# Feature sums of the first batch from a masked operand, and more of its outer products on GpSimd

## The chip, the cores and the metric

The kernel runs on one core of a Trainium2 chip. The metric is the device time of one execution in microseconds (us), the median of several runs. Engines are called as the profile calls them: PE (TensorE), DVE (VectorE), ACT (ScalarE), POOL (GpSimd), SP (SyncE, which only issues transfers here).

## The reference

Two layers, one behind the other. The first is an attention whose features are products of two small projections; the second is a gated feed-forward layer on its output.

```python
# q, k, v: (4, 4, 1088, 32); S1, S2: (8, 32)
def phi(x):
    a = np.einsum('rd,bhsd->bhsr', S1, x)
    b = np.einsum('rd,bhsd->bhsr', S2, x)
    return np.einsum('bhsi,bhsj->bhsij', a, b).reshape(*x.shape[:-1], r * r)
q_p, k_p = (phi(q), phi(k))
kv = np.einsum('bhsf,bhsd->bhfd', k_p, v)
z = np.sum(k_p, axis=2)
num = np.einsum('bhsf,bhfd->bhsd', q_p, kv)
den = np.einsum('bhsf,bhf->bhs', q_p, z)[..., None] + 1e-06
attn_out = num / den
# x: attn_out as (4352, 128)
gate = 1.0 / (1.0 + np.exp(-(x @ w_gate)))      # w_gate, w_val: (128, 1536)
out = (gate * (x @ w_val)) @ w_out              # w_out: (1536, 128)
```

The 64 features of a key are the outer product of its two projections a and b of 8 values each. z, the sum of these features over the 1088 keys of a head, is what the change computes in another way. S1, S2 and the weights arrive as 64-bit numbers and are narrowed to float32 on the chip.

## The kernel before

**Two phases that overlap.** The feed-forward layer is worked off in chunks of 512 tokens; each chunk is a sequence of twelve "waves" (`w1`, L501: gate and value products of one 128-wide slice of d_ff), each followed by the sigmoid on ACT (L509), the product g on DVE (L540) and, some waves later, the output products (L382, L338). The attention of batches 1 to 3 is put between the waves. The attention of batch 0 has nothing to hide behind: the first wave needs its result, so it stands alone at the start. All the code that the change touches belongs to this run-in of batch 0, apart from a few constants made ahead of it.

**What sets the order.** PE, DVE, ACT and POOL run under a manual schedule: every engine works through its instructions in the order in which the code emits them, and waits at each one for the semaphores of what it reads and of what it overwrites. So the place of a call in the source is its place in each engine's queue. Transfers are issued by SP, and a few by ACT.

**The run-in of batch 0, in the code's order.**
- `turn_k` transposes the keys; `kps(0)` projects them on PE, and DVE transposes the result back, for each pair of heads `pi` (L640, tile kab): 128 partitions of tokens, `NJK` = 9 token columns, and for each of the two heads of a pair the 8 values of a and the 8 of b.
- `ab` projects the queries on PE (tiles aps and bps); ACT copies one of the two (asb, L747), and `mult00` and `mult10` multiply them on DVE into qp (L756; one operand is in PSUM).
- `gram` multiplies kab by itself on PE: since z is the sum over the keys of a times b, z is the 8x8 block of kab-transposed times kab. The products of 9 token columns and two pairs go into PSUM tile gram (bank acc0). ACT copies 64 columns to gs (L662). POOL multiplies them by a mask e_m into gh, 128 x 32 (L664). `spread_z` then sums with one PE matmul against the constant e_sum (128 x 128; L676), which leaves every partition with a whole row of products; `mask_z` picks from it on DVE with the mask m_col (zm, L687) and a reduction (zb, L699). zb is z, in the layout that the denominator's matmul wants.
- `outer` forms the 64 features of the keys, kp, from kab by a product with two broadcast operands (L709), both in SBUF. Token column 8 of both pairs is made on POOL, behind gh; columns 0 to 4 by DVE; columns 5 to 7 by DVE after zb.
- `warm(512)` is a matmul of constants behind `spread_z` in PE's order (L260).
- `dn(0, 0, rest)`: PE computes the denominators dps from zb and qp (L1020). `rest` then has `kv0` (L836: kv from v and kp), the last DVE outers, the transpose dT of dps (L1031), the copy rc on ACT, and the turn of kv into nd (L871, L905, L922). The numerators nps follow (L1039), then the reciprocal, rb and the product xT (L1055 to L1060), which the first wave reads.
- `narrow` and `narrow_01` narrow the weights in steps on ACT (tail, L101; square, L117), POOL (cap, L97; head, L118) and DVE (head, L105 and L109; w_sb, L127), emitted between the steps above.

The calls that order this are in the main body:

```python
kps(0)
ab((0, 0, 0))
ab((0, 1, 0))
spread_z, mask_z = gram()
mult00 = ab(None, (0, 0, 0))
mult10 = ab(None, (0, 1, 0), (psm, "wave"))
```

Of the kernel before, what the change touches and what calls it, by code (L numbers as in the profile page):

```python
# [8 lines left out]
F32 = mybir.dt.float32  # L9
# [3 lines left out]
ALU = mybir.AluOpType  # L13
ACTF = mybir.ActivationFunctionType
MUL = ALU.mult

P = 128
# [3 lines left out]
def kernel(  # L21
# [12 lines left out]
    nc = tc.nc  # L34
# [234 lines left out]
    ident = const.tile([P, P], F32, tag="ident")  # L269
    make_identity(nc, ident)  # L270

    e_sum = const.tile([P, 2, R, R], F32, tag="e_sum")
    e_row = const.tile([P, R], F32, tag="e_row")
    e_m = const.tile([P, 2], F32, tag="e_m")
    id_m = ident.rearrange("p (g m x) -> p g m x", g=4, m=2)[:, :, :, :R]

    m_col = const.tile([P, 2, R], F32, tag="m_col")
    nc.gpsimd.memset(m_col, 0.0)
    for c in range(2):
        rows = slice(64 * c, 64 * c + 64)  # L280
        nc.vector.tensor_reduce(
            out=m_col[rows, c],
            in_=ident[rows].rearrange("p (k j) -> p j k", j=R),
            axis=mybir.AxisListType.X,
            op=ALU.add,
        )
    for t, x in (
        (e_row, id_m.rearrange("p g m x -> p x g m")),
        (e_m, id_m.rearrange("p g m x -> p m g x")),
    ):  # L290
        nc.vector.tensor_reduce(out=t, in_=x, axis=mybir.AxisListType.XY, op=ALU.add)
    nc.vector.tensor_copy(
        out=e_sum,
        in_=bass.AP(
            tensor=e_row.tensor,
            offset=e_row.offset,
            ap=[list(e_row.ap[0]), [0, 2], [1, R], [0, R]],
        ),
    )
    eps = const.tile([P, 1], F32, tag="eps")  # L300
    nc.gpsimd.memset(eps, 1e-6)
    zb = const.tile([P, H, 32], F32, tag="zb", name="zb")
# [317 lines left out]
    def kps(b):  # L620
        t = ps2.tile([P, 2, 512], F32, tag="two", name="kps")
        ts = [t[:, 0], t[:, 1]]
        turns = [(g, pi) for g in range(4) for pi in range(2)]

        if b == 0:
            ts[1] = pso.tile([P, TCH], F32, tag="acc1", name="kps1")
            turns.sort(key=lambda x: x[1])
        for g, pi in turns:
            rows = slice(64 * pi, 64 * pi + 64)
            nc.tensor.matmul(  # L630
                out=ts[pi][32 * g : 32 * g + 32, : NJK * 32],
                lhsT=sk[rows, :],
                rhs=kT_of[b][rows, KBASE[g] : KBASE[g] + NJK],
                start=True,
                stop=True,
            )

        KAB[b] = sbA.tile([P, 2, NJK, 32], F32, tag="kab", name="kab")
        for pi in range(2):
            nc.vector.transpose(  # L640
                out=KAB[b][:, pi].rearrange("p j c -> p (j c)"), in_=ts[pi][:, : NJK * 32]
            )
        KP[b] = sbA.tile([P, 2, NJK, 2, F], F32, tag="kp", name="kp", bufs=1)
# [3 lines left out]
    def gram():  # L647
        t = pso.tile([P, TCH], F32, tag="acc0", name="gram")
        for pi in range(2):
            for j in range(NJK):  # L650
                g = 32 * (j % 4)
                x = KAB[0][: 64 if j == 0 else P, pi, j]
                nc.tensor.matmul(
                    out=t[g : g + 32, 32 * pi : 32 * pi + 32],
                    lhsT=x,
                    rhs=x,
                    start=(j < 4),
                    stop=(j >= NJK - 4),
                    skip_group_check=True,
                )  # L660
        gs = const.tile([P, 2, 2, 2, R], F32, tag="gs")
        nc.scalar.copy(out=gs.rearrange("p a m x r -> p (a m x r)"), in_=t[:, :64])  # L662
        gh = const.tile([P, 2, 2, R], F32, tag="gh")
        nc.gpsimd.tensor_tensor(  # L664
            out=gh,
            in0=gs[:, :, :, 1],
            in1=bass.AP(
                tensor=e_m.tensor,
                offset=e_m.offset,
                ap=[list(e_m.ap[0]), [0, 2], [1, 2], [0, R]],  # L670
            ),
            op=MUL,
        )

        def spread_z():
            nc.tensor.matmul(  # L676
                out=t[:, 64 : 64 + H * R],
                lhsT=e_sum.rearrange("p c i j -> p (c i j)"),
                rhs=gh.rearrange("p a m r -> p (a m r)"),
                start=True,  # L680
                stop=True,
            )

        def mask_z():
            zm = const.tile([P, H, 2, R], F32, tag="zm")
            z0 = t[:, 64 : 64 + H * R]
            nc.vector.tensor_tensor(  # L687
                out=zm,
                in0=bass.AP(
                    tensor=z0.tensor, offset=z0.offset, ap=[list(z0.ap[0]), [R, H], [0, 2], [1, R]]  # L690
                ),
                in1=bass.AP(
                    tensor=m_col.tensor,
                    offset=m_col.offset,
                    ap=[list(m_col.ap[0]), [0, H], [R, 2], [1, R]],
                ),
                op=MUL,
            )
            nc.vector.tensor_reduce(  # L699
                out=zb[:, :, :2], in_=zm, axis=mybir.AxisListType.X, op=ALU.add  # L700
            )

        return spread_z, mask_z


    def outer(b, pi, j0=0, j1=NJK, eng=nc.vector):
        a0 = KAB[b][:, pi, j0:j1]
        ap = [list(a0.ap[0]), [2 * R, 2 * (j1 - j0)]]
        eng.tensor_tensor(  # L709
            out=KP[b][:, pi, j0:j1].rearrange("p j m (i l) -> p (j m) i l", i=R),  # L710
            in0=bass.AP(tensor=a0.tensor, offset=a0.offset, ap=ap + [[1, R], [0, R]]),
            in1=bass.AP(tensor=a0.tensor, offset=a0.offset + R, ap=ap + [[0, R], [1, R]]),
            op=MUL,
        )
# [6 lines left out]
    def ab(a_of=None, b_of=None, pool_b=None):  # L721

        mm = []
        if a_of is not None:
            aps = psm.tile([P, 2, 512], F32, tag="wave", name="aps")
            mm.append((a_of, aps, sa))
        if b_of is not None:
            pool, tag = (ps2, "two") if pool_b is None else pool_b
            bps = pool.tile([P, 2, 512], F32, tag=tag, name="bps")
            mm.append((b_of, bps, sb))  # L730
        for c in range(2):
            for m in range(2):
                for (bb, pr, n), dst, sx in mm:
                    h = 2 * pr + m
                    rows = slice(32 * h, 32 * h + 32)
                    t0, tn = q_chk[n]
                    nc.tensor.matmul(
                        out=dst[64 * c : 64 * c + 64, m, : 32 * tn],
                        lhsT=sx[rows, :],
                        rhs=qT_of[bb][rows, t0 : t0 + tn, c, :],  # L740
                        start=True,
                        stop=True,
                    )
        if a_of is not None:
            w = 32 * q_chk[a_of[2]][1]
            ASB[a_of] = sbA.tile([P, 2, 256], F32, tag="asb", name="asb", bufs=2)
            nc.scalar.copy(out=ASB[a_of][:, :, :w], in_=aps[:, :, :w])  # L747
        if b_of is not None:

            def mult():  # L750
                bb, pr, n = b_of
                if bb not in QP:
                    QP[bb] = sbA.tile([P, 2 * H * W1], F32, tag="qp", name="qp")
                t0, tn = q_chk[n]
                w = 32 * tn
                nc.vector.tensor_tensor(  # L756
                    out=half(QP[bb], n).rearrange("p (m c) w -> p c m w", m=2)[:, pr],
                    in0=bps[:, :, :w],
                    in1=ASB[b_of][:, :, :w],
                    op=MUL,  # L760
                )

            return mult
# [372 lines left out]
    sa, sb = sab  # L1136
    turn_q(0, 0)
    kps(0)
    ab((0, 0, 0))
    ab((0, 1, 0))  # L1140
    spread_z, mask_z = gram()
    mult00 = ab(None, (0, 0, 0))
    mult10 = ab(None, (0, 1, 0), (psm, "wave"))
    for pi in range(2):
        outer(0, pi, NJK - 1, NJK, eng=nc.gpsimd)
    for part in range(2):
        narrow_01(part, 0)
    spread_z()
    warm(512)
    for pi in range(2):  # L1150
        outer(0, pi, 0, 5)
    mult00()
    mult10()
    mask_z()


    def rest(turn, rc, dT):
        kv0([1, 2, 3, 4, 0])
        for pi in range(2):
            outer(0, pi, 5, NJK - 1)  # L1160
        kv0(range(5, NJK))
        turn()
        nt = rc.shape[1] - 1
        nc.scalar.activation(out=rc[:, :nt], in_=dT[:, :nt, :2], func=ACTF.Identity, bias=eps)
        kvd(0)
        narrow_01(0, 1)
        narrow_01(0, 2)
        ndt(0)
# [189 lines left out]
```

## Time and profile before

| what | value |
|---|---|
| median of 3 runs | 294.37 us (293.91 to 294.39) |
| profiled execution | 295.29 us, its span 293.5 us |
| PE busy, share of the span | 286.3 us, 98% |
| DVE, POOL, ACT busy | 187.4, 160.4, 92.1 us |
| first wave (L501) starts | 14.93 us into the span |

The span runs from the first to the last instruction that the profile saw; the execution's own time is 1.79 us longer. Busy times are modelled for PE: matmuls overlap, so a busy PE is not one at its peak. A line of the timeline gives the start, the length, the engine and line, the operation, output and inputs with their shapes, how many of them are merged, and in brackets the idle time ahead of the first and what ended it.

### The profile page before, as it was taken

The numbers are of one execution on the slowest core, as the hardware profiler recorded it, in microseconds if no ns is written. First come the engines' busy times: TensorE is split into PE (matmuls) and PEld (weight loads), VectorE is DVE, ScalarE is ACT, GpSimd is POOL, SyncE is SP. The second block draws the span as 40 slices with busy tenths as digits, with TensorE's granted clock in tenths as the row PEclk, the third lists the DMA queues.
The fourth block names the chain that finished last, engine by engine and source line by source line (L and its number), as shares of the span: only waits on it lengthen the run. The fifth ranks groups of instructions, "written<-read, shape, count | busy, mean of one in ns | idle before, by whom it ended". The sixth has DMA issues, their size and how long they took to land.

```text
span 293.5 us, 5784 instructions
## 1 busy us (share of the span) xinstructions
PE 286.3 (98%) x2276; PEld 155.4 (53%) x2276; DVE 187.4 (64%) x320; ACT 92.1 (31%) x168; POOL 160.4 (55%) x221
## 2 busy tenths in 40 slices
PE   8899999999899999999999999999999999999995
PEld 3444433346355455554555555554555555555895
DVE  6998789964847766677556695667336423552482
ACT  3557532322223322423223223313223222322321
POOL 2465553995345657546446498655456565656300
PEclk9999999999999999999999999999999999999999
DMA  7994531594700148436000574202000200020002
GB/s 215 328 354 105 134 95 57 127 172 133 220 22 0 20 128 167 127 83 181 9 0 2 129 171 105 41 0 38 1 2 0 36 2 0 0 32 6 2 3 53
DMA packets 28890, 24.23 MB, mean 83 GB/s; under 512 B 18560, under 2 KB 24064, under 8 KB 28864
## 3 DMA queue, kind: packets, MB, share of 16 engines
q1 hardware_dynamic: 28352, 23.10, 31.1%
q10 hardware_dynamic: 512, 0.77, 0.9%
q8 instruction: 18, 0.29, 0.4%
q14 instruction: 8, 0.07, 0.1%
HBM read 20.60 MB, written 3.26 MB: 81 GB/s over the span
## 4 chain that ended last, share of the span: by engine, by line
PE 76%; DMA 15%; SPq 3%; DVE 3%; POOL 1%; issue 1%; ACT 0%; POOLq 0%
PE wave L501 49%; PE prod L338 20%; DMA bq<-dq 7%; DMA v<-in_v_dram 3%; DMA w_in<-in_moe_w_out_dram 2%; PE moeout L408 2%; POOL head L118 1%; DMA kq<-in_k_dram 1%; PE moeout L382 1%; SPq L801 1%; PE nps L1214 1%; SPq L157 1%; DMA dq<-cq 1%; PE kvz L849 1%; DVE w_sb L127 1%
## 5 line engine op out<-in xcount | busy, mean ns | idle before, releaser
L501 PE MATMUL wave<-xT,w_sb 128*64 128x512 f32 (+3 forms) x820 | 210.7, 566 | 0.1
L501 PEld LDWEIGHTS wave<-xT,w_sb 128*64 128x64 f32 (+1 forms) x820 | 85.7, 140 | 63.1 <-issue 48.6
L509 ACT ACTIVATE sg<-wave 128x512 f32<-128x512 f32 x102 | 60.9, 597 | 170.7 <-PE wave L501 169.5
L540 DVE TENSOR_TENSOR g<-wave,sg 128x512 f32<-128x512 f32 x96 | 65.9, 686 | 75.7 <-ACT sg L509 74.5
L328 POOL TENSOR_TENSOR tsum<-g 128x256 f32<-128x256 f32 x84 | 66.9, 798 | 31.6 <-DVE g L540 31.4
L328 POOL TENSOR_TENSOR tsum<-g,tsum 128x256 f32<-128x256 f32 x42 | 34.2, 814 | 57.4 <-DVE g L540 57.2
L338 PE MATMUL prod<-tsum,ws 128*64 128x256 f32 x252 | 62.8, 381 | 0.0
L338 PEld LDWEIGHTS prod<-tsum,ws 128*64 128x64 f32 x252 | 31.2, 137 | 16.2 <-issue 11.8
L338 PE MATMUL prod<-g,w_sb 128*64 128x256 f32 x168 | 34.9, 383 | 0.0
L328 POOL TENSOR_TENSOR tsum<-tsum,g 128x256 f32<-128x256 f32 x42 | 32.7, 779 | 3.3
L338 PEld LDWEIGHTS prod<-g,w_sb 128*64 128x64 f32 x168 | 15.7, 137 | 18.2 <-issue 15.4
L338 PE MATMUL prod<-tsum,w_sb 128*64 128x256 f32 x84 | 25.4, 384 | 0.0
L338 PE MATMUL prod<-g,ws 128*64 128x256 f32 x84 | 25.0, 379 | 0.0
L118 POOL TENSOR_TENSOR head<-head,tail 128x384 int32<-128x384 int32 (+2 forms) x14 | 13.3, 953 | 17.8 <-DVE head L109 11.6
L338 PEld LDWEIGHTS prod<-g,ws 128*64 128x64 f32 x84 | 11.5, 137 | 3.7
L829 DVE TENSOR_TENSOR qp<-qp,bq 128x1152 f32<-128x1152 f32 (+1 forms) x7 | 9.1, 1296 | 6.4 <-DMA a<-dq 6.4
L382 PE MATMUL moeout<-g,w_sb 128*128 128x512 f32 (+1 forms) x28 | 12.6, 607 | 0.3 <-DVE w_sb L127 0.3
L338 PEld LDWEIGHTS prod<-tsum,w_sb 128*64 128x64 f32 x84 | 10.9, 137 | 2.9 <-issue 1.9
L709 DVE TENSOR_TENSOR kp<-kab 128x1152 f32<-128x1152 f32 (+2 forms) x10 | 10.9, 1111 | 0.0
L440 DVE TENSOR_TENSOR res<-prod,other 64x512 f32<-64x512 f32 (+1 forms) x14 | 7.6, 543 | 3.1 <-ACT other L434 3.1
L533 DVE TENSOR_TENSOR g<-wave,sg 128x512 f32<-128x512 f32 x6 | 6.5, 1087 | 4.7 <-ACT sg L509 4.7
L475 DVE STREAM_TRANSPOSE o_sb<-res 64x512 f32<-64x512 f32 x14 | 9.5, 686 | 0.0
(121 smaller groups left out, 201.5 us busy)
## 6 DMA issues: line engine op xcount, KB each, us to landing
qp<-dq SPq DMA_DIRECT2D x7, 576.0 KB
bq<-dq SPq DMA_DIRECT2D x14, 288.0 KB
kq<-in_k_dram SPq DMA_DIRECT2D x3, 544.0 KB
kq<-in_q_dram SPq DMA_DIRECT2D x3, 544.0 KB
w_in<-in_moe_w_out_dram SPq DMA_DIRECT2D x6, 256.0 KB
w_in<-in_moe_w_gate_dram SPq DMA_DIRECT2D x5, 256.0 KB
w_in<-in_moe_w_val_dram SPq DMA_DIRECT2D x5, 256.0 KB
out_dram<-o_sb SPq DMA_DIRECT2D x20, 64.0 KB
```

Of the source, the lines that this page charges most:

```text
L118: nc.gpsimd.tensor_tensor(out=head, in0=head, in1=tail, op=ALU.add)
L328: nc.gpsimd.tensor_tensor(out=t[:, u], in0=in0, in1=in1, op=ALU.subtract)
L338: nc.tensor.matmul(out=out, lhsT=lhsT, rhs=rhs, start=start, stop=stop, skip_group_check=True)
L382: nc.tensor.matmul(out=moe["acc"][d], lhsT=w_sb[:, 2, j, d], rhs=g[:, jj], start=(j == 0), stop=(j == NJ - 1),)
L440: nc.vector.tensor_tensor(out=out, in0=in0, in1=in1, op=op)
L475: nc.vector.transpose(out=o_sb[:64, d].rearrange("p t x -> p (t x)"), in_=r[:, 1 + 2 * d : 3 + 2 * d].rearrange("p u x -> p (u x)"),)
L501: nc.tensor.matmul(out=wv[d, which, jj * tw + o : jj * tw + o + tp], lhsT=w_sb[:, which, j0 + jj, d], rhs=xT[:, t0 + o : t0 + o + tp], sta ...
L509: nc.scalar.activation(out=sg, in_=wv[:, 0], func=ACTF.Sigmoid)
L533: nc.vector.tensor_tensor(out=g.rearrange("p (j u s y) -> p j y u s", j=2, u=2, y=4), in0=wv[:, 1].rearrange("p (j y u s) -> p j y u s", j ...
L540: nc.vector.tensor_tensor(out=g, in0=wv[:, 1], in1=sg, op=MUL)
L709: eng.tensor_tensor(out=KP[b][:, pi, j0:j1].rearrange("p j m (i l) -> p (j m) i l", i=R), in0=bass.AP(tensor=a0.tensor, offset=a0.offset, ...
L829: nc.vector.tensor_tensor(out=q0, in0=q0, in1=half(BQ[b], n), op=MUL)
```

## The change

Three things are changed. gh becomes the whole masked operand: POOL spreads the 8 products of each head over 64 columns (i, j) with the mask e_row, and gh is 128 x 256 instead of 128 x 32. `spread_z` sums it by eight small matmuls, one for each head and half, with gh as the stationary operand and a constant e_c of two columns as the moving one; each writes 64 partitions and two columns. ACT copies these eight columns to zb, so zm, the reduction on DVE and the constants e_sum, e_m and m_col are gone. And POOL makes token columns 7 and 8 of kp instead of column 8 alone, ahead of gh in its order, straight behind `kps(0)`; DVE's last outers are columns 5 and 6. The call of `spread_z` now stands ahead of the first narrowing step, which puts the copy zb ahead of the tails (L101) in ACT's order.

```diff
-    e_sum = const.tile([P, 2, R, R], F32, tag="e_sum")
...
+    id_m = ident.rearrange("p (g m x) -> p m x g", g=4, m=2)[:, :, :R]
+    e_row = const.tile([P, 2, 2, R], F32, tag="e_row")
+    for a in range(2):
+        nc.vector.tensor_reduce(out=e_row[:, a], in_=id_m, axis=mybir.AxisListType.X, op=ALU.add)
+    e_c = const.tile([P, 2, 2], F32, tag="e_c")
+    nc.vector.memset(e_c, 0.0)
     for c in range(2):
...
+        nc.vector.memset(e_c[:, c, c : c + 1], 1.0)
...
-        gh = const.tile([P, 2, 2, R], F32, tag="gh")
+        gh = const.tile([P, H, R, R], F32, tag="gh")
+        g0 = gs[:, :, :, 1]
         nc.gpsimd.tensor_tensor(
             out=gh,
-            in0=gs[:, :, :, 1],
+            in0=bass.AP(
+                tensor=g0.tensor, offset=g0.offset, ap=[list(g0.ap[0]), [2 * R, H], [0, R], [1, R]]
+            ),
             in1=bass.AP(
-                tensor=e_m.tensor,
...
+                tensor=e_row.tensor,
+                offset=e_row.offset,
+                ap=[list(e_row.ap[0]), [R, H], [1, R], [0, R]],
             ),
             op=MUL,
         )
 
         def spread_z():
-            nc.tensor.matmul(
-                out=t[:, 64 : 64 + H * R],
-                lhsT=e_sum.rearrange("p c i j -> p (c i j)"),
...
-        def mask_z():
...
+            for h in range(H):
+                for c in range(2):
+                    nc.tensor.matmul(
+                        out=t[64 * c : 64 * c + 64, 64 + 2 * h : 66 + 2 * h],
+                        lhsT=gh[:, h].rearrange("p i j -> p (i j)"),
+                        rhs=e_c[:, c],
+                        start=True,
+                        stop=True,
+                        skip_group_check=True,
+                    )
+            nc.scalar.copy(
+                out=zb[:, :, :2], in_=t[:, 64 : 64 + 2 * H].rearrange("p (h c) -> p h c", c=2)
+            )
...
     kps(0)
+    for pi in range(2):
+        outer(0, pi, NJK - 2, NJK, eng=nc.gpsimd)
     ab((0, 0, 0))
     ab((0, 1, 0))
-    spread_z, mask_z = gram()
+    spread_z = gram()
     mult00 = ab(None, (0, 0, 0))
     mult10 = ab(None, (0, 1, 0), (psm, "wave"))
-    for pi in range(2):
-        outer(0, pi, NJK - 1, NJK, eng=nc.gpsimd)
+    spread_z()
     for part in range(2):
         narrow_01(part, 0)
-    spread_z()
     warm(512)
     for pi in range(2):
         outer(0, pi, 0, 5)
     mult00()
     mult10()
-    mask_z()
...
         for pi in range(2):
-            outer(0, pi, 5, NJK - 1)
+            outer(0, pi, 5, NJK - 2)
```

More of the change, by code (lines that the diff above doesn't have):

```diff
@@ L270 @@
     make_identity(nc, ident)
-    e_sum = const.tile([P, 2, R, R], F32, tag="e_sum")
[L273 to L278, printed above, removed]
-    for c in range(2):
[L280 to L299, printed above, removed]
+    id_m = ident.rearrange("p (g m x) -> p m x g", g=4, m=2)[:, :, :R]
[4 more added lines that the diff above has]
+    nc.vector.memset(e_c, 0.0)
+    for c in range(2):
+        nc.vector.memset(e_c[:, c, c : c + 1], 1.0)
     eps = const.tile([P, 1], F32, tag="eps")
@@ L662, in gram @@
         nc.scalar.copy(out=gs.rearrange("p a m x r -> p (a m x r)"), in_=t[:, :64])
-        gh = const.tile([P, 2, 2, R], F32, tag="gh")
+        gh = const.tile([P, H, R, R], F32, tag="gh")
+        g0 = gs[:, :, :, 1]
         nc.gpsimd.tensor_tensor(
             out=gh,
-            in0=gs[:, :, :, 1],
+            in0=bass.AP(
+                tensor=g0.tensor, offset=g0.offset, ap=[list(g0.ap[0]), [2 * R, H], [0, R], [1, R]]
+            ),
             in1=bass.AP(
-                tensor=e_m.tensor,
-                offset=e_m.offset,
-                ap=[list(e_m.ap[0]), [0, 2], [1, 2], [0, R]],
+                tensor=e_row.tensor,
+                offset=e_row.offset,
+                ap=[list(e_row.ap[0]), [R, H], [1, R], [0, R]],
             ),
@@ L675, in spread_z @@
         def spread_z():
-            nc.tensor.matmul(
-                out=t[:, 64 : 64 + H * R],
-                lhsT=e_sum.rearrange("p c i j -> p (c i j)"),
-                rhs=gh.rearrange("p a m r -> p (a m r)"),
-                start=True,
-                stop=True,
-            )
-        def mask_z():
[L685 to L703, printed above, removed]
+            for h in range(H):
[10 more added lines that the diff above has]
+                out=zb[:, :, :2], in_=t[:, 64 : 64 + 2 * H].rearrange("p (h c) -> p h c", c=2)
+            )
+        return spread_z
     def outer(b, pi, j0=0, j1=NJK, eng=nc.vector):
```

## The prediction

> **What bounds the kernel now.** I read the page's busy shares and slices first, then the busy time by stage, then the timeline of the stage that the change touches.
>
> ```profile
> PE 286.3 (98%) x2276; PEld 155.4 (53%) x2276; DVE 187.4 (64%) x320; ACT 92.1 (31%) x168; POOL 160.4 (55%) x221
> ```
>
> ```profile
> 6.80:10.80 4.00, 3.46 (x76) 1.59 (x74) 3.97 (x9) 1.97 (x5) 1.94 (x5) 1.00 1.11 299
> 10.80:15.00 4.20, 3.33 (x100) 1.99 (x100) 4.10 (x12) 2.42 (x7) 1.42 (x3) 1.00 1.03 349
> 15.00:22.50 7.50, 7.16 (x27) 3.40 (x28) 7.10 (x16) 4.01 (x8) 4.69 (x8) 1.00 1.06 345
> 22.50:48.00 25.50, 25.44 (x82) 10.51 (x84) 20.89 (x40) 12.57 (x25) 14.90 (x19) 1.00 0.39 109
> 100.00:200.00 100.00, 100.00 (x845) 53.67 (x842) 66.29 (x102) 28.94 (x50) 62.62 (x76) 1.00 0.37 86
> ```
>
> After each window's length stand the busy times of PE, PEld, DVE, ACT and POOL. From 22.5 us on PE has no holes, apart from 0.92 us at 74.4 to 75.8, where denj waits for a DMA. In the run-in, 6.8 to 15.0, VectorE is the full engine: 3.97 of 4.00 and 4.10 of 4.20 us. So whatever delays or advances the first wave (L501, at 14.93) moves the whole PE-bound rest with it, one to one. The waits of 15 to 22.5 are DVE, ACT, POOL and PE on each other; the last weight slices land some microseconds ahead of their use (w_in 2 at 16.5, first read at 20.3), so no transfer holds that stretch in place.
>
> The run-in on VectorE, POOL and PE (timeline of each engine):
>
> ```profile
> 7.55 1.52 DVE L709 TENSOR_TENSOR kp<-kab 128x640 f32<-128x640 f32 x2
> 9.05 1.29 DVE L756 TENSOR_TENSOR qp<-bps,asb 128x512 f32<-128x512 f32 x2
> 10.26 0.21 DVE L687 TENSOR_TENSOR zm<-gram,m_col 128x64 f32<-128x64 f32 x1
> 10.50 0.22 DVE L699 TENSOR_REDUCE zb<-zm 128x8 f32<-128x64 f32 x1
> 10.64 1.10 DVE L709 TENSOR_TENSOR kp<-kab 128x384 f32<-128x384 f32 x2
> 11.66 0.44 DVE L1031 STREAM_TRANSPOSE dT<-dps 128x256 f32<-128x256 f32 x1
> ```
>
> ```profile
> 9.22 0.41 PE L676 MATMUL gram<-gh,e_sum 128*128 128x32 f32 x2 [0.28 <-POOL gh L664]
> 9.46 1.11 PE L260 MATMUL warm<-const-float32-1.0 128*128 128x512 f32 x2
> 10.78 0.64 PE L1020 MATMUL dps<-qp,zb 128*32 128x256 f32 x8 [0.21 <-DVE zb L699]
> ```
>
> From dT (11.66) to the first wave, every step follows from dT: rc, its reciprocal, rb, the narrowing of w_sb, xT. VectorE is full from 11.66 to 14.88, so the shift of dT is the shift of the wave. dT needs both VectorE free and dps done; dps ends 0.64 after it starts, so dT can start 0.70 after dps starts. Today VectorE decides: dps would allow 11.48.
>
> **Who may use SBUF.** These POOL and DVE lines carry the forecast:
>
> ```profile
> 8.68 0.48 POOL L664 TENSOR_TENSOR gh<-gs,e_m 128x32 f32<-128x32 f32 x1 [2.43 <-ACT gs L662]
> 9.13 0.76 POOL L709 TENSOR_TENSOR kp<-kab 128x128 f32<-128x128 f32 x2
> ```
>
> ```profile
> 39.32 1.35 DVE L829 TENSOR_TENSOR qp<-qp,bq 128x1152 f32<-128x1152 f32 x1
> ```
>
> ```profile
> 39.57 1.96 POOL L118 TENSOR_TENSOR head<-head,tail 128x384 int32<-128x384 int32 x1 [1.12 <-DVE head L109]
> ```
>
> gh has 32 elements and yet takes 0.48 us, ending 0.10 after the DVE outer product ends (9.07). The add of 39.57 takes 1.96 where its like take 1.00, ending 0.86 after qp ends (40.67). In both, POOL stood still while DVE ran an operation with two SBUF operands. The two POOL outers of 9.13 run beside L756, which reads PSUM, and take 0.40 each, undisturbed. The other way round, L109 on DVE took 1.01 instead of 0.56 at 16.98 because a POOL add ran until 17.58. [...] the one held back ends about 0.13 early against its own length (0.86 for 1.00)[...].
>
> On length, [...] 0.592 us for 192 elements (L324) and 0.722 for 256 (L328), 2.03 ns per element. On matmuls, [...] here the last 16 gram passes start in fours, 32 ns apart.
>
> **The change, part by part.**
>
> *Set-up.* Of the DVE reductions m_col, e_row, e_m and the copy e_sum (1.45 us together), two reductions and three memsets remain; a POOL memset goes. Nothing: VectorE waits for s_in until 3.73 anyway, and is through at 2.69 today.
>
> *Off VectorE.* zm and zb (10.26 to 10.64) go, and the last outers fall from 384 to 256 elements: by 0.93 ns per element (0.784 for 640, 0.546 for 384) 0.12 each. Together 0.66 us less before dT, if dps lets dT come.
>
> *Onto POOL, ahead of gh.* Two outers of 256 elements instead of two of 128 behind gh, and gh itself is 256 instead of 32. Length of each: 0.40 plus 128 x 2.03 ns is 0.66; a plain 256 takes 0.727. I take 0.69, with 0.60 and 0.80 as ends. POOL follows DVE by 0.15 to 0.17 (L109 12.73, L118 12.88), so the first starts at 7.26 (first kab) + 0.16 = 7.42, ahead of the DVE outer at 7.55, and they share the lock:
> - POOL outer 1: 7.42 to 8.11. DVE outer 1, held until 8.11, ends at 8.11 + 0.78 - 0.13 = 8.76.
> - DVE outer 2 is issued before outer 1 ends. In such a case (o_sb and kp at 168 us) a waiting POOL add got the lock only after both. So DVE outer 2 ends at 8.76 + 0.74 = 9.50.
> - POOL outer 2 ends at 9.50 + 0.69 - 0.13 = 10.06; gh, beside the PSUM-reading L756, runs 10.02 to 10.71.
>
> Were POOL let in between the two DVE outers, gh would end at 10.54; were DVE first at 7.55, at 10.94. I take 10.71, against 9.17 today: 1.54 later. L756 moves by 0.43 and ends at 10.79, which nobody feels.
>
> *On PE.* One matmul (2 passes, 128 columns, loads 0.11 apart) becomes eight (16 passes of 64 columns). A 64-column load taken as half of 0.11, two column groups together: 8 x 0.055 = 0.44 us; ends 0.25 and 0.90 (no overlap). Behind it in PE's order stands warm (512 columns), then dps. Today the first warm pass starts 0.25 after the first gh load, and dps could follow 1.19 after that load; now it becomes 1.43. With gh at 10.71 the load starts at 10.76 and dps at 12.19, 1.41 later than today's 10.78.
>
> *zb.* Eight columns copied by ACT instead of two DVE steps, about 0.2 (gs takes 0.21), beside the 1.1 us of warm: nothing. Queued behind it on ACT are the two tails (L101), late by some 1.5 us; POOL's first head needs them only after dT. If that cover goes, the tails' 0.76 us would stand ahead of rc.
>
> *POOL's caps* (L97), now behind gh, move from 10.07 to 10.67 or later; DVE's L105 needs them after dT. Nothing. No DMA moves.
>
> *Sum.* dT at 12.19 + 0.70 = 12.89, against 11.66: +1.23. VectorE then idles ahead of dT: the 0.66 that it gained is lost in a wait for dps. The second path, kvz to nps, moves by 1.41 but has 0.25 of slack ahead of xT (nps over at 14.16, xT at 14.47): +1.16, just covered. The wave moves to about 16.16. The profiled execution would take 295.29 + 1.23 = 296.5 (its span is 293.5, 1.79 lie around it; it stands 0.92 above the median of the runs). From the median: 294.37 + 1.23 = 295.6. With lengths of 0.60, the early order and 0.25 for PE the shift is +0.6; with 0.80, the late order and 0.90 it is +2.2.
>
> **The rivals.**
>
> *No contention, faster.* If POOL's two outers ran beside DVE's, gh would end at about 7.42 + 3 x 0.66 - 0.07 = 9.33, dps start at 10.81 and dT at 11.51: -0.15, 294.2. With PE at 0.25 it is -0.34. It decides once gh ends before 9.3; it ends at -0.66 (293.7), where VectorE itself is the bound again, and that needs gh at 8.8. For it speaks that 0.66 us really leaves the full engine; against it stand gh's 0.48 and the 1.96 of L118.
>
> *Hidden later.* The shift is real at the first wave but the 0.92 us wait of denj takes it in: +0.3, 294.7. Against: its transfer starts from cq, which PE makes, so it moves too.
>
> *The PE clock.* PE would stand idle from 8.94 to 10.76. [...] the granted clock is 1.00 in every window today, so no trace here shows such a fall. [...]
>
> **How the numbers follow.** A measurement of this kernel can tell about 0.2% (0.59 us) from no change. Lock chain 0.81 (0.71 slower by more than that, 0.10 within it); no contention 0.13 (0.07 faster, where the POOL operations also turn out shorter than assumed, 0.06 within); hidden later 0.04 (0.03 within, 0.01 slower); clock 0.02, slower. Faster 0.07, same 0.19, slower 0.74. The range goes from just under the short ends of the chain to its long ones, 294.5 to 296.4; it leaves out most of the no-contention case and the clock.
>
> **What would show it.** Right: POOL outers or DVE outers of 1.2 us and more between 7.4 and 10; gh ending near 10.7; warm ending near 12.2; VectorE idle ahead of dT, released by PE dps; the first wave near 16.2; stages after 22.5 as long as now. Wrong: POOL and DVE outers both at their own length and gh over by 9.4, or a first wave before 15.

## The result, and the profile after

The changed kernel is slower: median 297.29 us of 16 executions, against 295.50 of 16 of the kernel before, ratio 1.0068 (95% interval 1.0046 to 1.0091). Run again beside the experiments it gave 297.63 against 295.03, ratio 1.0060 (1.0035 to 1.0084). Ratios are formed from the fast executions of both kernels, so they are not the quotients of the medians beside them. The profiled execution took 297.28, its span 295.5: 2.0 us more than before. The forecast was 295.6, in 294.5 to 296.4: the right direction, too small.

The timeline of each engine in the run-in, first POOL, then DVE, then PE (start, length, work, and in brackets the idle time ahead and what ended it):

```profile
8.11 1.79 POOL L679 TENSOR_TENSOR kp<-kab 128x256 f32<-128x256 f32 x2 [1.91 <-DVE kab L620]
9.86 1.20 POOL L645 TENSOR_TENSOR gh<-gs,e_row 128x256 f32<-128x256 f32 x1
11.03 0.79 POOL L97 TENSOR_SCALAR cap<-w_in 128x256 f32<-128x256 f32 x2
```

```profile
7.54 0.85 DVE L620 STREAM_TRANSPOSE kab<-kps 128x288 f32<-128x288 f32 x2 [1.10 <-PE kps L610]
8.31 2.27 DVE L679 TENSOR_TENSOR kp<-kab 128x640 f32<-128x640 f32 x2
10.50 1.27 DVE L726 TENSOR_TENSOR qp<-bps,asb 128x512 f32<-128x512 f32 x2
11.70 0.74 DVE L679 TENSOR_TENSOR kp<-kab 128x256 f32<-128x256 f32 x2
13.44 0.45 DVE L1001 STREAM_TRANSPOSE dT<-dps 128x256 f32<-128x256 f32 x1 [1.00 <-PE dps L990]
```

```profile
9.02 0.69 PE L707 MATMUL bps<-qT,s 32*64 32x256 f32 x16
11.11 0.63 PE L661 MATMUL gram<-e_c,gh 128*64 128x2 f32 x16 [1.41 <-POOL gh L645]
11.68 1.13 PE L260 MATMUL warm<-const-float32-1.0 128*128 128x512 f32 x2
12.73 0.64 PE L990 MATMUL dps<-qp,zb 128*32 128x256 f32 x8
```

The chain of the forecast is all there. Its first part is called the lock, or the port lock, here: a name for turns that the lengths show; what makes POOL and DVE take them was not shown. Where POOL ran beside the DVE outers, which have two SBUF operands, the two took turns: the two DVE outers take 2.27 us instead of 1.52, POOL's second outer takes 1.21 where its first takes 0.62, and gh 1.20. DVE, full before, stands idle for 1.00 ahead of dT, released by PE's dps; and dps stands behind gh, the sum and warm. PE itself has a hole of 1.41 ahead of the sum.

Before the chain begins, this execution is already later than the earlier profile: the first transpose kab starts at 7.54 instead of 6.78. Here PE ran slowly for longer: the two constant matmuls ahead of kps took 1.22 together, against 0.70, and the trace's record of the clock, whose first entry is 1.00, begins at 6.93 instead of 4.03. In two of the later profiles (the changed kernel again, and the one without warm) kab starts still later, at 7.74 and 7.76, for another reason: the transpose of the keys waited 0.90 and 0.88 for their transfer. In the others it starts at 6.8 to 7.1. Neither cause lies in code that was changed, but all three late starts are among the eight profiles with the new constants and none among the three with the old ones; so few don't exclude a link. I measure from the start of kab. dT comes 5.90 us after it, against 4.88 before: +1.02. xT, the first wave's input, comes 8.72 after it, against 7.69: +1.03. The profile's 2.0 us are these 1.03, the late start's 0.76, and some 0.36 of a longer wait of denj for its transfer, less small differences:

```profile
PE denj L948 <- DMA b<-dq: 1.3, 2, 0.8
```

(The waits of PE after 24 us: in total, times, longest; before it was 0.9, and over all the profiles it is 0 to 1.8.) One execution cannot say what the other half of the 2.0 is in all executions. The list of executions can: each has a mean granted PE clock, as a share of the full one. The values fall into two groups, 0.998 and more or 0.994 and less; one stretch of 3.41 us at a clock of 0.50, as it is seen below, lowers the mean of 294 us by 0.006. Of the 34 of the changed kernel, 25 lie under 0.996. Of the kernel before, none of 62 beside the first experiments, 4 of 38 beside the second, 1 of 19 beside the last; for its 16 beside the result no clock is on record. Within the changed kernel the executions with a low clock are the longer ones: medians 297.66 (11) against 297.09 (5) at first, 297.75 (14) against 296.07 (4) when run again.

### The profile page after: what moved, and what is told of

It is laid out like the page before. It is cut to its first block, busy times and chain, and to the rows that moved or that the text cites. A ratio compares the mean times of both kernels' runs of the same rounds, so it can differ in the third digit from the quotient of the medians.

```text
span 295.5 us, 5811 instructions
## 1 busy us (share of the span) xinstructions
PE 287.5 (97%) x2290; PEld 155.7 (53%) x2290; DVE 187.6 (63%) x318; ACT 92.2 (31%) x169; POOL 162.7 (55%) x220
## 4 chain that ended last, share of the span: by engine, by line
PE 72%; DMA 15%; DVE 5%; SPq 2%; POOL 2%; issue 1%; ACT 1%; POOLq 0%; DVEq 0%
PE wave L481 47%; PE prod L318 20%; DMA bq<-dq 5%; DMA w_in<-in_moe_w_val_dram 4%; DMA v<-in_v_dram 2%; POOL head L118 2%; DMA kq<-in_q_dram 2%; DMA out_dram<-o_sb 1%; DVE w_sb L127 1%; PE moeout L362 1%; DVE head L109 1%; SPq L771 1%; PE nps L1183 1%; SPq L330 1%; DMA dq<-cq 1%
## 5 line engine op out<-in xcount | busy, mean ns | idle before, releaser
L308 POOL TENSOR_TENSOR tsum<-g 128x256 f32<-128x256 f32 x84 | 67.9, 810 | 30.7 <-DVE g L520 30.5
```

Of the source, the lines that this page charges most:

```text
L308: nc.gpsimd.tensor_tensor(out=t[:, u], in0=in0, in1=in1, op=ALU.subtract)
```

## The experiments

All ratios are to the kernel before, run on the same chip in the same session. "After kab" is the time from the start of the first kab transpose in the profiled execution.

**The changed kernel again** (a control, unaltered).

> The changed kernel unaltered, beside the others on one chip. Two-part theory (chain 1.0 us[...], plus PE's clock falling to half for one or two windows because PE idles 1.4 us ahead of the sum): ratio 1.005 to 1.008, most executions with a mean clock of 0.995 or less. Chain alone: 1.0035, clocks of 0.998 and more.

Ratio 1.0060 (1.0035 to 1.0084); 14 of 18 executions had a mean clock under 0.996, most at 0.992 to 0.994 or 0.988. The two-part theory (the chain, and PE's clock) stands. The profiled execution, the longest of them (301.20), has a clock of 0.988 and shows two falls: one behind the hole of 1.41 ahead of the sum, one far outside the run-in, behind a wait of denj of 1.45. Busy times by stage (PE, PEld, DVE, ACT, POOL; then PE's granted clock):

```profile
8.95:12.36 3.41, 2.00 (x51) 1.30 (x50) 3.41 (x6) 0.96 (x5) 3.08 (x4) 1.00 1.05 355
12.36:15.77 3.41, 3.41 (x66) 1.87 (x68) 1.43 (x5) 0.86 (x3) 0.00 (x0) 0.50 1.05 371
77.21:80.63 3.42, 1.58 (x28) 0.55 (x32) 2.02 (x3) 0.60 (x1) 0.28 (x1) 1.00 0.35 93
80.63:84.04 3.41, 3.41 (x46) 1.42 (x32) 2.08 (x5) 1.01 (x1) 2.59 (x4) 0.50 1.04 295
```

gh ends 3.52 after kab, as in the first profile, but xT comes 10.29 after it instead of 8.72: the fall in the run-in cost this execution 1.57.

**The new sum alone.** POOL makes one column, behind gh.

```diff
     kps(0)
-    for pi in range(2):
-        outer(0, pi, NJK - 2, NJK, eng=nc.gpsimd)
...
+    for pi in range(2):
+        outer(0, pi, NJK - 1, NJK, eng=nc.gpsimd)
     spread_z()
...
-            outer(0, pi, 5, NJK - 2)
+            outer(0, pi, 5, NJK - 1)
```

> The new feature sum alone: POOL makes one column of kp, behind gh, as in the kernel before. Port-lock theory: gh (256 elements) waits only for the second DVE outer and ends about 0.5 us later than before, measured from the transposes kab; with the longer PE step dps starts some 0.55 later and dT 0.4 later: about +0.4 us, ratio 1.001. Theory that the eight small matmuls on PE are what costs: most of the loss stays, ratio 1.004 or more. Clock theory (PE's idle time ahead of the sum lowers its clock in some executions): the hole in front of the sum is about 0.8 instead of 1.4 us, so fewer executions with a mean clock under 0.995, ratio 1.001 to 1.004.

Ratio 1.0018 (1.0004 to 1.0032), 2 of 22 clocks under 0.996. The timeline of POOL:

```profile
8.96 0.87 POOL L645 TENSOR_TENSOR gh<-gs,e_row 128x256 f32<-128x256 f32 x1 [2.62 <-ACT gs L642]
9.79 0.77 POOL L679 TENSOR_TENSOR kp<-kab 128x128 f32<-128x128 f32 x2
```

gh waits only for the rest of the second DVE outer and takes 0.87. dT comes 5.15 after kab, +0.27, where the port-lock theory said about +0.4; the small matmuls are not what costs most.

**The outers alone**, in front, with the old sum.

```diff
     kps(0)
+    for pi in range(2):
+        outer(0, pi, NJK - 2, NJK, eng=nc.gpsimd)
...
-    for pi in range(2):
-        outer(0, pi, NJK - 1, NJK, eng=nc.gpsimd)
...
-            outer(0, pi, 5, NJK - 1)
+            outer(0, pi, 5, NJK - 2)
```

> The POOL outers alone: two columns of kp on POOL, first in its order, with the old sum (gh of 32 elements, one matmul, zm and zb on DVE). Port-lock theory: POOL's two outers and DVE's two take turns, each held for 0.5 to 0.6 us; gh ends about 1.5 us after its place in the kernel before, less 0.4 for its 32 elements; zm and zb come after L756 and dT is about 0.5 us later: ratio 1.0015 to 1.002. Theory that the sum is what costs: 1.000 or below, since VectorE has 0.24 us less to do. Clock theory: a hole of 1 us and more on PE ahead of the sum, ratio 1.003 or more with mean clocks under 0.995.

Ratio 1.0021 (1.0008 to 1.0033), 1 of 22 clocks under 0.996. The timeline of POOL:

```profile
7.44 1.79 POOL L709 TENSOR_TENSOR kp<-kab 128x256 f32<-128x256 f32 x2 [1.14 <-DVE kab L640]
9.19 0.82 POOL L664 TENSOR_TENSOR gh<-gs,e_m 128x32 f32<-128x32 f32 x1
```

gh, 32 elements again, now takes 0.82 because it waits for the second DVE outer from its beginning. dT comes 5.38 after kab, +0.50: as the port-lock theory said. The two parts alone make 0.77 of the 1.02. At gh they add up: it ends 0.39 and 0.74 later alone, 1.13 together. At dT they don't, mostly because dps had 0.18 to spare in the kernel before, which each part alone uses up first. Neither brings the low clocks, although this kernel's PE waits 1.02 us for gh; there the clock theory had expected them.

**DVE's order turned**, so that POOL's three operations meet no DVE operation with two SBUF operands.

```diff
+    mult00()
+    mult10()
     for pi in range(2):
         outer(0, pi, 0, 5)
-    mult00()
-    mult10()
```

> The changed kernel with DVE's order turned: the two products of L726 that read PSUM first, the two outer products of 640 elements behind them. POOL's three operations keep their place. Port-lock theory: POOL's second outer (1.21 us in the changed kernel) and gh (1.20) then take 0.6 to 0.7 us each, as the first (0.62) does, and gh ends about 1.0 us earlier against the first kab transpose; the DVE outers, with POOL's caps beside them, keep or exceed their length. If the broadcast operands are what makes POOL slow, they stay at 1.2. The time is no better, since DVE then reaches dT late.

The timeline of POOL:

```profile
7.66 1.21 POOL L679 TENSOR_TENSOR kp<-kab 128x256 f32<-128x256 f32 x2 [1.41 <-DVE kab L620]
9.00 0.63 POOL L645 TENSOR_TENSOR gh<-gs,e_row 128x256 f32<-128x256 f32 x1
```

The two outers and gh take 0.63 each; the same instructions took 0.62, 1.21 and 1.20. That settles the lock: it is not the broadcast operands that make POOL slow, but the DVE outers beside it. gh ended 2.53 after kab instead of 3.52. dT came 5.62 after kab (a single execution, 295.34 us).

**PE's hole filled**: 512 and 256 columns of constants ahead of the sum, nothing else.

```diff
...
+    fill = psm.tile([P, 2, 512], F32, tag="wave", name="warm")
+    warm(512, 256, t=fill)
     spread_z()
     for part in range(2):
         narrow_01(part, 0)
-    warm(512)
+    warm(512, t=fill)
```

> The changed kernel with two matmuls of constants (512 and 256 columns, about 1.3 us) in PE's order ahead of the sum, where PE otherwise waits for gh. Nothing that the chain waits for is touched. Port-lock chain alone: as the changed kernel, ratio 1.0068 within its interval. Clock theory: PE no longer has the hole of 1.4 us, mean clocks return to those of the kernel before, and only the chain's own 1.0 us is left: ratio 1.003 to 1.004.

Ratio 1.0036 (1.0024 to 1.0049), and no clock of 16 under 0.996. The timeline of PE:

```profile
8.98 1.56 PE L261 MATMUL warm<-const-float32-1.0 128*128 128x512 f32 x4
10.48 0.63 PE L662 MATMUL gram<-e_c,gh 128*64 128x2 f32 x16
11.04 1.13 PE L261 MATMUL warm<-const-float32-1.0 128*128 128x512 f32 x2
12.10 0.64 PE L991 MATMUL dps<-qp,zb 128*32 128x256 f32 x8
```

dT comes 5.91 after kab, as in the changed kernel (5.90): the chain is untouched, and work that computes nothing takes back about half of the loss. What is left, 1.16 us between the medians (295.91 and 294.75), is about the chain's 1.03. The changed kernel itself was not run beside this one; the next kernel, with the same hole of 1.41, was, and there 11 of 15 clocks are low.

**No warm behind the sum.**

```diff
         narrow_01(part, 0)
-    warm(512)
```

> The changed kernel without the 512-column matmul of constants between the sum and dps. Chain theory (dT waits for dps, dps for PE's order behind gh): dps starts about 0.9 us earlier, at the end of L756, and dT too; of the 1.0 us lost in the run-in about 0.1 is left: ratio 1.003 to 1.004 if something else makes up the rest of the 0.0068, 1.0005 if not. Clock theory: PE is idle more, more executions with a clock under 0.995, no gain or a further loss.

Ratio 1.0050 (1.0032 to 1.0067), 11 of 15 clocks under 0.996. For the chain this run says little, because the profiled execution shows the clock's fall itself. Busy times by stage and PE's granted clock, as above, and the timeline of PE:

```profile
8.40:11.80 3.40, 1.99 (x69) 1.37 (x68) 3.40 (x5) 1.19 (x3) 3.40 (x5) 1.00 1.09 297
11.90:15.20 3.30, 2.98 (x84) 2.31 (x80) 2.46 (x9) 1.18 (x4) 0.67 (x2) 0.50 1.07 374
15.30:18.70 3.40, 2.67 (x24) 1.57 (x25) 2.63 (x8) 2.00 (x6) 1.69 (x4) 1.00 1.06 375
```

```profile
11.34 0.63 PE L661 MATMUL gram<-e_c,gh 128*64 128x2 f32 x16 [1.41 <-POOL gh L645]
12.29 1.08 PE L990 MATMUL dps<-qp,zb 128*32 128x256 f32 x8 [0.32 <-ACT zb L669]
13.15 2.15 PE L806 MATMUL kvz<-kp,v 128*32 128x64 f32 x72
```

After a stretch with 1.99 of 3.40 us busy, PE ran at a clock of 0.50 from 11.87 to 15.28; dps took 1.08 instead of 0.64 and kvz 2.15 instead of 1.19. In this execution, as in that of the changed kernel again, the late keys had made another hole, of 0.81 (there 0.76), ahead of kps, one stretch of 3.41 us earlier; whether it has a part in the fall is not shown.

**Warm moved ahead of the sum**: hole filled and path to dps cleared.

```diff
...
+    warm(512, 256)
     spread_z()
...
-    warm(512)
```

> The changed kernel with the constants' matmuls moved: 512 and 256 columns ahead of the sum, in the hole where PE waits for gh, and none between the sum and dps. Two-part theory: the clock stays up, and dps starts right behind L756's end, about 0.9 us earlier than with the matmul in between; dT then comes 5.0 us after the first kab transpose begins, against 4.9 before the change: ratio 1.000 to 1.001. If the matmul between sum and dps is not on the path: as with the filled hole alone, 1.0036. If PE's order does not matter to the clock: 1.003 or more, with clocks under 0.995.

Ratio 1.0010 (0.9982 to 1.0039), 1 of 14 clocks under 0.996. dT comes 5.25 after kab instead of 5.90, 0.25 later than expected, because dps now waits for the zb copy:

```profile
11.36 0.64 PE L991 MATMUL dps<-qp,zb 128*32 128x256 f32 x8 [0.32 <-ACT zb L670]
```

Compared with the run above, whose order behind the sum is the same and whose clock fell, xT comes 8.07 after kab instead of 9.37. So one stretch of 3.41 us at a clock of 0.50 cost 1.3 us here, against the 1.57 between the changed kernel's own two profiles.

**A hole in the kernel before**: its own warm taken away, its chain untouched.

```diff
     spread_z()
-    warm(512)
```

> The kernel before the change without its 512-column matmul of constants: dps waits for zb anyway, so the chain is not touched, but PE has a hole of some 1.2 us there. Clock theory: in a part of the executions the clock falls to half for a window, mean clock 0.994, and these are 1 to 2 us longer; ratio 1.001 to 1.005. If the hole does nothing to the clock: 1.000, clocks as before.

Ratio 1.0005 (0.9978 to 1.0032): inconclusive. PE waited 1.15 us there, and 4 of 14 clocks lay under 0.996, against 4 of 38 of the kernel before beside it. That points the clock theory's way but is too few.

**A version meant to beat both**: the sum alone, warm ahead of it, POOL's column behind the caps.

```diff
-    for pi in range(2):
-        outer(0, pi, NJK - 2, NJK, eng=nc.gpsimd)
...
+    warm(512)
     spread_z()
     for part in range(2):
         narrow_01(part, 0)
-    warm(512)
+    for pi in range(2):
+        outer(0, pi, NJK - 1, NJK, eng=nc.gpsimd)
...
-            outer(0, pi, 5, NJK - 2)
+            outer(0, pi, 5, NJK - 1)
```

> A version meant to beat both: the new sum on PE, with the 512-column matmul of constants ahead of it (so that PE has no hole and dps follows the sum directly), and POOL's one column of kp placed behind gh and the first two caps[...]. Port-lock and clock theory: DVE is the bound again; without zm and zb dT comes some 4.6 us after the first kab transpose begins, against 4.9 in the kernel before: 0.2 to 0.3 us less, ratio 0.999 to 1.000, mean clocks of 0.998 and more. If POOL's caps still meet DVE's last outers: dT at 4.9, ratio 1.000 to 1.001.

It doesn't beat the kernel before: ratio 1.0022 (1.0002 to 1.0042), medians 294.69 and 294.62. dT came 4.81 after kab, 0.07 earlier than before, but not at the expected 4.6. Timeline of DVE and POOL:

```profile
10.36 0.55 DVE L679 TENSOR_TENSOR kp<-kab 128x384 f32<-128x384 f32 x1
10.38 0.80 POOL L679 TENSOR_TENSOR kp<-kab 128x128 f32<-128x128 f32 x1
10.82 0.76 DVE L679 TENSOR_TENSOR kp<-kab 128x384 f32<-128x384 f32 x1
```

POOL's column was meant to run beside the DVE products that read PSUM. Behind the caps it starts only as DVE's last outers do; DVE's second was held for 0.2, and dps waits 0.32 for zb besides. Why the ratio lies above 1 with a run-in no longer than before is open; two of the 14 executions (296.40 and 297.92) weigh on it.

## Why the prediction was right and wrong

**Where the time would be lost: right.** The turns of POOL and DVE (2.27 us for two DVE outers instead of 1.52), gh's lateness, PE's order sum, warm, dps, and DVE's gain turned into a wait of 1.00 are what the trace shows, and the turned DVE order shows the turns as the cause (gh 0.63 instead of 1.20).

**The sum of the chain: 1.23 forecast, 1.02 measured at dT.** Counted from kab, gh ended at 3.52 (forecast 3.93); dps started at 5.19 (5.41). Three terms were off. POOL's 256 elements take 0.63, not 0.69. POOL's second outer was let in between the two DVE outers, which I had named but not taken; the order was then POOL, DVE, POOL, DVE, gh, and gh was held for the whole second DVE outer. And dps came 1.62 after the first load of gh, not 1.43. The sixteen passes start over 0.44 us, as estimated, but the first warm pass follows the last of them only 0.13 later, 0.08 after its place in the sum, and dps came 1.05 after the first warm pass, where the sum has 0.94.

**What hid what: right.** The tails behind zb on ACT, the caps behind gh and the set-up cost nothing at dT; the kvz path stayed covered, since dT and xT moved by the same 1.02 and 1.03. The shift reached the end about one to one: 1.16 us between the medians with the hole filled. The wait of denj did not take it in: it was 1.3 in this profile, against 0.9.

**The step that failed: the rival of the PE clock, given 0.02 and put at nothing in the sum.** Its ground was that "the granted clock is 1.00 in every window today". That was a fact of a kernel whose holes there are 0.28 and 0.21 us, so it said nothing about the new one; that the clock stays up through the longer gap, 8.94 to 10.76 by the forecast, was my estimate, and no trace showed it. The runs contradict it: a hole of 1.41 us, with 2.00 of 3.41 us busy around it, is followed by a clock of 0.50 in both profiles that show a fall in the run-in, and 25 of 34 executions of the changed kernel have a low mean clock. Nor was it a rival: it comes on top of the chain. Filling the hole brings 1.0036, which is the forecast of 1.0042 within its interval, and no low clock. As an estimate, a fall of 1.3 to 1.6 us in 25 of 34 executions makes 1.0 to 1.2 us on average, about what the 1.0068 has beyond the chain's 1.03. So the hole, through the clock, is the missing half; that the falls at denj and the late starts have a smaller part is not excluded.

**The base, the second term that was off.** The forecast stood on three executions with a median of 294.37; over the sessions the kernel before gave 294.6 to 295.5. On 295.50 the forecast shift would have given 296.7. That alone put the number outside the range, whatever the clock did. The other way round, the 1.79 us between the medians, counted from 294.37, would have ended at 296.2, inside the range, with nearly half of it from a cause that the forecast had left out.

## What to carry to other kernels

Before work moves to GpSimd, look which DVE instructions will run beside it: in these traces two-operand SBUF work took turns with it, and was stretched by up to the other's length (0.78 to 1.24 on DVE, 0.62 to 1.21 on POOL), while DVE work that reads PSUM left it alone (0.63). Where a change makes PE wait, price the wait twice: once on the chain (1.02 us here), and once for the clock of the work behind it (1.3 and 1.57 us where it fell to 0.50); here a matmul of constants belonged inside the hole, ahead of the waiting matmul (ratio 1.0010), and not behind it (1.0060), where it only lengthened the path. A granted clock of 1.00 in one profile says nothing of the list of executions (the changed kernel's first profile has 1.00, and 25 of its 34 executions lie under 0.996); read the mean clock of each.

## What the runs showed of the hardware that I had not expected

- PE's clock fell to 0.50 for one stretch of 3.41 us after a stretch of 3.41 us that was 59% busy with one hole of 1.41 us; the same is seen twice (the changed kernel again, and the one without warm), and once more at denj, after a stretch 46% busy with a hole of 1.45. By the longest hole ahead of the sum or dps, the shares of executions with a mean clock under 0.996 are: 0.28 (the kernel before), 5 of 119; filled, with 0.32 at most, 2 of 44; 0.66 us, 2 of 22; 1.02, 1 of 22; 1.15, 4 of 14; 1.41, 36 of 49. It rises steeply between 1.0 and 1.4 us.
- Where in time the hole falls seems to count. In the changed kernel again the clock's changes lie whole multiples of 3.41 us apart: the record begins at 5.53 and changes at 12.36, 15.77, 80.63 and 84.04. In the first profile of the changed kernel it begins at 6.93. With this spacing, an estimate from these times, a boundary at 10.34 cuts the hole of 1.41 into 0.64 and 0.77; the stretches on both sides were 79% and 77% busy, and the clock stayed up:

```profile
6.93:10.34 3.41, 2.69 (x84) 1.18 (x68) 2.80 (x4) 1.24 (x3) 2.23 (x3) 1.00 1.11 313
10.34:13.75 3.41, 2.64 (x67) 1.69 (x71) 2.41 (x6) 0.86 (x3) 1.48 (x3) 1.00 1.06 373
13.75:17.17 3.42, 2.67 (x67) 1.50 (x57) 3.28 (x11) 2.32 (x7) 1.74 (x3) 1.00 1.07 376
```

  In the two profiles with the fall the hole lay whole inside one such stretch. That would explain why the same kernel falls in some executions and not in others; it fits these three profiles and was not tested. Nor is the busy share the whole of it: the kernel before without its warm was busy for 1.98 of 3.41 us (58%) from 9.07 to 12.48, with holes of 0.28 and 1.15, and its clock stayed up. The exact rule is open.

- In the changed kernel POOL got its turn between two DVE instructions of which the second was issued (9.33) before the first had ended (9.41). In the kernel before, at 168 us, it had to wait for both (a tsum of 2.36 us, where the median of its like is 0.73). A wait of the second instruction's own is not what decides: at 168 us the second had none, but neither had it in the version meant to beat both, and there POOL was let in, again ahead of a second that was issued (10.82) before the first had ended (10.91); the three lines stand with that experiment. What decides is open.
